# Division right behind the second products, GpSimd's subtractions in quarters, one-hot rows in one instruction, routing's rows of steps waiting by name

## The chip, the cores and the metric

The kernel runs on one core of one Trainium2 chip. Its time is the device time of one execution in microseconds (us). A core has engines that each run their own instructions in order and wait for one another through semaphores. TensorE (PE) does matrix products and transposes, VectorE (DVE) and ScalarE (ACT) work element by element, GpSimd (POOL) does the same and issues the gathers and scatters, and SyncE (SP) issues the other transfers (DMA). Loading of weights into TensorE is shown as PEld.

## The reference, cut to what matters

The first half is an attention in which each position sees its neighbours at a distance under 16 and one summary for each of 24 blocks of 32 positions. The second half sends each of the 3072 resulting rows through one of eight experts. Which expert that is depends on the rows before it.

```
# attention: B, H, S, D = 4, 8, 768, 64
k_sum = k.reshape(B, H, 24, 32, D).max(axis=3)
v_sum = v.reshape(B, H, 24, 32, D).mean(axis=3)
scores = scale * [q @ k.T where |i - j| < 16, q @ k_sum.T + log(32)]
a = exp(scores - max); a = a / (sum(a) + 1e-9)
x = (a @ [v, v_sum]) as B, S, 512
# routing and experts: E = 8, F = 1024
logits = x @ w_gate; local = sigmoid(x @ w_local)
e = argmax(logits) where s == 0 or local < 0.5, else the expert of the row before
out = softmax(logits)[e] * (relu(x @ w1[e]) @ w2[e])
```

## The kernel before, in words

**Attention.** The 4 blocks (one for each batch element) have 4 pairs of heads each. Such a pair is handled in two groups of 3 x 128 queries, so there are 32 groups, counted by `G`. The loop in `attention` is a pipeline by hand: in one turn `s_mm(G)` computes the scores (L251, L257), `t_stage(G - 2)` transposes the exponentials of two groups earlier (L278), `a_mm(G - 3)` multiplies with the values (L289), and `s_exp(G)` finds the row maximum on DVE (`nm`, L264) and exponentiates on ACT (L268). `a_norm` divides by the sum of the weights in three DVE instructions (L300, L302, L304). It takes group `G - 4` and stands ahead of `nm` of the same turn. The product's result has a single buffer in PSUM (bank "a"), so `a_mm` of one group waits until `a_norm` of the group before has read it. GpSimd prepares the scaled key windows (L216), folds the values (L209), writes the key summaries (L219) and spreads the value summaries (L228). `sum_v` (L223) turns value sums that DVE made (L204).

**Routing.** When the rows of a block are complete, they are transposed and multiplied with the gate's weights (L450, L468), and a row of small DVE steps with a few PE steps between them finds each row's expert and its place in that expert's list. These rows of steps are Python generators. `small(n)` issues up to n steps from the first two of them between two parts of the attention; `flow(dt)` does the same during the experts' products, by planned times (`C_DVE` for a step on DVE, `C_LAT` for its latency, `C_LONG` for a long one). At the end of a block's steps six instructions write one-hot rows `A` of 128 x 128 (L581). They are weights of later matrix products: `early(j)` (L700) finds which rows the slots 2j and 2j + 1 hold, `early_p(j)` (L727) their gate weights, and `finish` does so for the other slots, first with a product for four slots (L852 with 8 columns), then one that makes the words for the experts' numbers (L917), one for 32 slots (L852 with 64 columns), and the gate weights of 36 slots (L938). Block 3's routing and `finish` stand beside the experts' first three pairs.

**Experts.** A slot is 128 rows of one expert; slots are worked on in pairs (pairs 0 to 2 are the early ones). The rows are gathered by an indirect DMA (L960), transposed (L971), and multiplied by w1 (96 products of "first" kind, L1015 to L1017) and w2 (48 of "second" kind, L988 to L990). Every operand is a sum of a high and a low part, hence three products for each. ACT casts the high part of a weight (`h`, L951), and DVE or GpSimd subtracts it from the weight for the low part (`l`, L954, pieces of 128 x 1024). The slots of the next pair are gathered and transposed during the second products of a pair. The result is scaled by the gate weight (L997, L1000) and scattered (L1001). A store whose gate weight has not been planned yet issues routing's steps until it has, at that place (`while self.have_p <= i: self.small(1, True)`).

The engines' orders are fixed when the program is built. Only the loading and splitting of an expert's weights from pair 3 on depends on values read at run time.

Of the kernel before, what the change touches and what calls it, by code (L numbers as in the profile page):

```python
# [57 lines left out]
C_T, C_PE, C_WAIT, C_LONG, C_DVE, C_LAT, AHEAD = 0.65, 0.8, 0.3, 0.9, 0.17, 0.05, 1.5  # L58
# [4 lines left out]
class Kernel:  # L63
    def __init__(self, ctx, tc, qT, kT, vT, vW, maskc, identc, wgc, w1, w2, c32c, cb16c, out):
# [3 lines left out]
        self.t, self.q = 0.0, 0.0  # L68
        self.qT, self.kT, self.vT, self.vW = qT, kT, vT, vW
# [74 lines left out]
    def attention(self, tick, last):  # L144
        nc, tc, ident = self.nc, self.tc, self.ident
        with ExitStack() as ctx:
# [45 lines left out]
            for load, n in ((load_k, 1), (load_q, 1), (load_v, 0), (load_w, 0), (load_v, 1), (load_w, 1), (load_q, 2)):  # L192
                load(n)
# [18 lines left out]
            def windows(n, eng=nc.gpsimd, t0=0, t1=NW):  # L212

                src = kp[n % 2][:, 64 * t0:64 * t0 + 1]
                win = bass.AP(src.tensor, src.offset, [src.ap[0], (64, t1 - t0), (1, WL)])
                eng.tensor_scalar(out=kb[n % 2][:, t0:t1, 0:WL], in0=win, scalar1=0.125, scalar2=1.0, op0=ALU.mult, op1=ALU.mult)  # L216
# [75 lines left out]
            def a_norm(G):  # L292
# [8 lines left out]
                self.small(1)  # L301
                nc.vector.reciprocal(out=dn, in_=dn)  # L302
                self.small(1)
# [8 lines left out]
            windows(0, nc.vector, 0, NW // 2)  # L312
# [6 lines left out]
            for G in range(last_g + LA):  # L319
# [8 lines left out]
                if G < last_g and G % GP == 0 and G:  # L328
                    sum_v(G // GP, self.spare[:, 1, 0:P])
# [3 lines left out]
                if LA + 1 <= G <= last_g:  # L333
                    a_norm(G - LA - 1)
                tick(G, 3)
                if G < last_g:
                    s_exp(G)
                    self.small(3)
# [6 lines left out]
                if LA <= G:  # L345
                    a_mm(G - LA)
                if G < last_g:
# [15 lines left out]
                    else:  # L363
                        if n == 0:
                            sum_v(0, self.bank("t")[:, 0:P])
# [4 lines left out]
                        spread_v(n)  # L370
# [3 lines left out]
                else:  # L374
                    a_norm(G - LA)
                tick(G, 1)
                if G < last_g:
                    self.small(4, True)
                else:
                    self.flow(C_T)  # L380
# [8 lines left out]
    def wait(self):  # L389
        while len(self.steps) > 1:  # L390
            yield "WAIT"
# [92 lines left out]
    def route(self, b):  # L484
# [56 lines left out]
        v.tensor_tensor_scan(out=s2, data0=c["keep"], data1=o2, initial=0.0, op0=ALU.mult, op1=ALU.add)  # L541
        yield "PE"
# [35 lines left out]
        for u in range(NU):  # L578
            if u % 2 == 0:
                yield "DVE"  # L580
            v.tensor_scalar(out=self.A[:, b * NU + u, :], in0=c["iota128"], scalar1=lanf[:, u:u + 1],  # L581
                            scalar2=None, op0=ALU.is_equal)
# [21 lines left out]
    def second(self):  # L604
# [15 lines left out]
        v.scalar_tensor_tensor(out=cnt, in0=self.er, scalar=2.0 * P, in1=cnt, op0=ALU.mult, op1=ALU.max)  # L620
        yield "DVE"
# [16 lines left out]
        v.tensor_scalar(out=self.adj[:, 2], in0=self.is1, scalar1=-2.0, scalar2=7.0, op0=ALU.mult, op1=ALU.add)  # L638

    def gate_p(self, b0, b1):  # L640
# [30 lines left out]
        for i in range(3):  # L671
            yield "DVE"
            v.tensor_copy(out=p3[:, :, i, 0], in_=r)
            if i < 2:
                yield "DVE"
                v.tensor_tensor(out=r, in0=r, in1=p3[:, :, i, 0], op=ALU.subtract)

    def early(self, j, ef=None, places=None):
# [3 lines left out]
        n = self.early_b(j) * NU  # L682
        ef, places = ef or self.e0f, places or (2.0 * j, 2.0 * j + 1)
# [20 lines left out]
        for i in range(2):  # L704
            yield "DVE"
            v.scalar_tensor_tensor(out=self.lb[:, 0:n], in0=in0[:, :, i], scalar=64.0, in1=self.lb[:, 0:n], op0=ALU.mult, op1=ALU.add)

# [43 lines left out]
    def finish(self):  # L751
# [5 lines left out]
        nci = wk.tile([P, E], I32, name="nci")  # L757
        q = wk.tile([P, E], F32, name="q")
# [166 lines left out]
        yield from self.gate_p(B - 1, B)  # L925
        n = SLOTS - EARLY
# [22 lines left out]
    def split(self, which, c0, c1, src, eng):  # L949
        hi, lo = self.hi[which][:, c0:c1], self.lo[which][:, c0:c1]  # L950
        self.nc.scalar.copy(out=hi, in_=src)  # L951
        if eng is self.nc.vector:
            self.dve(1.1)
        eng.tensor_tensor(out=lo, in0=src, in1=hi.bitcast(F32), op=ALU.subtract)  # L954
# [389 lines left out]
```

## Time and profile before

| | |
|---|---|
| median of 3 runs | 497.64 us (493.22 to 499.40) |
| the profiled execution | 497.38 us, its span 495.6 us |
| mean granted TensorE clock | 0.957 |
| PE, PEld busy | 448.0 us (90%), 389.0 us (78%) |
| DVE, ACT, POOL busy | 285.2 us (58%), 216.4 us (44%), 190.1 us (38%) |
| moved by DMA | 92.04 MB, 186 GB/s in the mean |

Times in the profile count from the span's first instruction. Busy shares are of the span. The granted clock is what the throttle allowed TensorE in a stretch of time, 1.00 being full speed. In a row of the timeline the first number is the start, the second the duration, and a bracket at the end shows how long the engine had sat idle and what ended that. In a row of waits the numbers are the total, the number of waits and the longest.

### The profile page before, as it was taken

The page shows a single profiled execution, that of the slowest core. Times are in us where ns is not written, and L with a number is a line of the kernel's source. Part 1 is how long each engine was busy: PE and PEld are TensorE (multiplying, and loading weights), DVE is VectorE, ACT ScalarE, POOL GpSimd, SP SyncE. Part 2 cuts the span into 40 slices and gives each one's busy share as a digit, 9 for nine tenths or more (in the row PEclk, how much of TensorE's full clock was granted, in tenths as well). Part 3 has the DMA queues.
Part 4 walks back from the last instruction along what each step waited for, and adds up shares of the span by engine and source line. Part 5 has one row for each costly group of instructions (what it writes and reads, how often), then busy time and mean ns, then how long its engine had stood idle before and what let it go on. Part 6 is the DMA issues. An engine that isn't in the chain of part 4 may idle for free. (4 is left out here: it accounts for less than half of the span.)

```text
span 495.6 us, 11918 instructions
## 1 busy us (share of the span) xinstructions
PE 448.0 (90%) x4400; PEld 389.0 (78%) x4400; DVE 285.2 (58%) x623; ACT 216.4 (44%) x478; POOL 190.1 (38%) x152
## 2 busy tenths in 40 slices
PE   6899988878779999889899999999999999999990
PEld 5687776767567789688799998989879898977980
DVE  4686698777663756965522223158686226777610
ACT  3698876677535322702110201054556116274500
POOL 2685553373401230631102111146477204566720
PEclk9799999979879999979999999999999999999996
DMA  8999799678212084016402010119498503847840
GB/s 317 404 370 375 285 321 395 239 256 341 88 56 75 1 296 173 21 65 231 197 1 85 23 65 28 58 43 323 145 324 280 197 33 110 309 165 253 291 162 26
DMA packets 23622, 92.04 MB, mean 186 GB/s; under 512 B 2927, under 2 KB 3567, under 8 KB 19440
## 3 DMA queue, kind: packets, MB, share of 16 engines
q1 hardware_dynamic: 18752, 76.11, 42.2%
q0 software_dynamic: 4640, 14.68, 8.7%
q8 instruction: 41, 0.67, 0.5%
q14 instruction: 45, 0.37, 0.2%
q10 hardware_dynamic: 144, 0.20, 0.1%
HBM read 78.40 MB, written 13.11 MB: 185 GB/s over the span
## 5 line engine op out<-in xcount | busy, mean ns | idle before, releaser
L1015 PE MATMUL bs<-xT,h 128*128 128x256 f32 x384 | 110.6, 288 | 0.0
L1016 PE MATMUL bs<-xT,h 128*128 128x256 f32 x384 | 109.5, 285 | 0.5 <-DVE xT L966 0.5
L1017 PE MATMUL bs<-xT,l 128*128 128x256 f32 x384 | 109.6, 285 | 0.1
L1021 ACT ACTIVATE hT<-bs 128x512 fp32r<-128x512 f32 x48 | 28.7, 598 | 131.8 <-PE bs L1017 127.7
L960 POOL DMA_INDIRECT xg<-x_dram,gidx x32 | 34.8, 1089 | 127.5 <-POOLq L1191 57.7
L988 PE MATMUL ba<-h,hT 128*128 128x512 f32 x192 | 77.7, 405 | 0.4
L1023 DVE SCALAR_TENSOR_TENSOR hT<-bs,hT 128x512 fp32r<-128x512 f32 x48 | 33.0, 690 | 77.7 <-ACT hT L1021 66.8
L1016 PEld LDWEIGHTS bs<-xT,h 128*128 128x128 f32 x384 | 74.5, 194 | 1.1 <-DVE xT L966 0.7
L990 PE MATMUL ba<-h,hT 128*128 128x512 f32 x192 | 75.1, 391 | 0.0
L989 PE MATMUL ba<-l,hT 128*128 128x512 f32 x192 | 75.0, 391 | 0.0
L1015 PEld LDWEIGHTS bs<-xT,h 128*128 128x128 f32 x384 | 74.5, 194 | 0.7 <-issue 0.2
L1017 PEld LDWEIGHTS bs<-xT,l 128*128 128x128 f32 x384 | 74.4, 194 | 0.5 <-DVE l L954 0.5
L954 DVE TENSOR_TENSOR l<-stg,h 128x1024 fp32r<-128x1024 f32 x35 | 67.9, 1949 | 11.3 <-ACT h L951 8.1
L268 ACT ACTIVATE pr<-bs,nm 128x120 f32<-128x120 f32 x192 | 52.0, 372 | 25.2 <-DVE nm L264 24.8
L951 ACT CAST h<-stg 128x1024 fp32r<-128x1024 f32 x56 | 57.2, 1052 | 11.3 <-PE ba L990 8.2
L954 POOL TENSOR_TENSOR l<-stg,h 128x1024 fp32r<-128x1024 f32 x21 | 51.4, 2467 | 20.4 <-ACT h L951 20.4
L1001 POOL DMA_INDIRECT out_dram<-yo,sidx x26 | 31.1, 1197 | 59.1 <-DVE yo L1000 40.2
L988 PEld LDWEIGHTS ba<-h,hT 128*128 128x128 f32 x192 | 36.1, 188 | 8.0 <-ACTq L1191 0.6
L289 PE MATMUL ba<-vw,pt 120*64 120x65 f32 x768 | 33.0, 241 | 10.3 <-DVE xs L304 5.9
L990 PEld LDWEIGHTS ba<-h,hT 128*128 128x128 f32 x192 | 36.0, 188 | 7.8
L289 PEld LDWEIGHTS ba<-vw,pt 120*64 120x64 f32 x768 | 28.9, 153 | 15.7 <-issue 11.6
L989 PEld LDWEIGHTS ba<-l,hT 128*128 128x128 f32 x192 | 36.2, 189 | 6.2
(236 smaller groups left out, 672.3 us busy)
## 6 DMA issues: line engine op xcount, KB each, us to landing
stg<-in_w SPq DMA_DIRECT2D x32, 1024.0 KB, 5.7
vw<-in_vW SPq DMA_DIRECT2D x16, 780.0 KB, 4.5
kp<-in_kT SPq DMA_DIRECT2D x16, 384.0 KB, 6.3
q<-in_qT SPq DMA_DIRECT2D x16, 384.0 KB, 6.7
vt<-in_vT SPq DMA_DIRECT2D x16, 384.0 KB, 7.3
x_dram<-xs SPq DMA_DIRECT2D x8, 768.0 KB, 9.9
wst<-in_w SPq DMA_DIRECT2D x8, 512.0 KB, 8.4
xg<-x_dram,gidx POOLq DMA_INDIRECT x32, 8.4
```

What stands on the lines that cost most here:

```text
L268: nc.scalar.activation(out=pr[:, h, u, :], in_=sp[:, h, u, :], func=AF.Exp, bias=nm[:, h, u:u + 1], scale=1.0)
L289: nc.tensor.matmul(out=ap[64 * c:64 * c + 64, u, h, :], lhsT=pt[:, h, u, 64 * c:64 * c + 64], rhs=vw[n % 3][0:W, 2 * (NG * g + u) + c, h, ...
L951: self.nc.scalar.copy(out=hi, in_=src)
L954: eng.tensor_tensor(out=lo, in0=src, in1=hi.bitcast(F32), op=ALU.subtract)
L960: self.nc.gpsimd.indirect_dma_start(out=t, out_offset=None, in_=rows, in_offset=bass.IndirectOffsetOnAxis(ap=self.gidx[:, i:i + 1], axis=0))
L988: nc.tensor.matmul(out=ps, lhsT=ah, rhs=wh, start=first, stop=False)
L989: nc.tensor.matmul(out=ps, lhsT=ah, rhs=wl, start=False, stop=False)
L990: nc.tensor.matmul(out=ps, lhsT=al, rhs=wh, start=False, stop=last)
L1015: nc.tensor.matmul(out=ps[:, j], lhsT=wh, rhs=xh, start=(k == 0), stop=False)
L1016: nc.tensor.matmul(out=ps[:, j], lhsT=wh, rhs=xl, start=False, stop=False)
L1017: nc.tensor.matmul(out=ps[:, j], lhsT=wl, rhs=xh, start=False, stop=(k == KT - 1))
L1023: nc.vector.scalar_tensor_tensor(out=l, in0=ps, scalar=0.0, in1=h.bitcast(F32), op0=ALU.max, op1=ALU.subtract)
```

## The change

In the attention, `a_norm(G - 3)` now stands right behind `a_mm(G - 3)`, and no routing steps are slipped between its three instructions. `small` issues 3 + 2 + 3 steps in a turn, where it was 3 + 2 + 4 and the two of `a_norm`. The value sums of the first pair of heads are turned in the turns 2 and 3, and half of the first key windows is scaled by ACT. The one-hot rows of a block become one instruction of 128 x 768, which the planner counts as long. A GpSimd subtraction of 128 x 1024 becomes four of 128 x 256. Four planned costs are larger. Rows of steps wait by name (`until`) for what other rows of steps have done.

```
-C_T, C_PE, C_WAIT, C_LONG, C_DVE, C_LAT, AHEAD = 0.65, 0.8, 0.3, 0.9, 0.17, 0.05, 1.5
+C_T, C_PE, C_WAIT, C_LONG, C_DVE, C_LAT, AHEAD = 0.65, 0.8, 0.3, 1.1, 0.19, 0.1, 1.5
...
-            for load, n in ((load_k, 1), (load_q, 1), (load_v, 0), (load_w, 0), (load_v, 1), (load_w, 1), (load_q, 2)):
+            for load, n in ((load_k, 1), (load_v, 0), (load_q, 1), (load_w, 0), (load_v, 1), (load_w, 1), (load_q, 2)):
...
+                if eng is nc.scalar:
+                    eng.activation(out=kb[n % 2][:, t0:t1, 0:WL], in_=win, func=AF.Copy, scale=0.125)
...
                 nc.vector.tensor_scalar(out=dn, in0=ap[:, :, :, D:D + 1], scalar1=1e-9, scalar2=None, op0=ALU.add)
-                self.small(1)
                 nc.vector.reciprocal(out=dn, in_=dn)
-                self.small(1)
...
-                if LA + 1 <= G <= last_g:
-                    a_norm(G - LA - 1)
+                if G in (2, 3):
+                    sum_v(G - 2, self.bank("t")[:, 0:P])
+                    spread_v(G - 2)
...
-                    self.small(3)
+                    self.small(3, True)
...
                     a_mm(G - LA)
+                    a_norm(G - LA)
...
-                        spread_v(n)
+                        if n > 1:
+                            spread_v(n)
...
-                    self.small(4, True)
+                    self.small(3, True)
...
+    def until(self, *names):
+        while not self.done.issuperset(names):
+            yield "WAIT"
...
+        yield from self.until(("counts", b))
...
-        for u in range(NU):
-            if u % 2 == 0:
-                yield "DVE"
-            v.tensor_scalar(out=self.A[:, b * NU + u, :], in0=c["iota128"], scalar1=lanf[:, u:u + 1],
-                            scalar2=None, op0=ALU.is_equal)
+        if b < B - 2:
+            self.done.add(("counts", b + 1))
+        yield "LONG"
+        v.tensor_tensor(out=self.A[:, ts, :], in0=c["iota128"].unsqueeze(1).to_broadcast([P, NU, P]),
+                        in1=lanf.unsqueeze(2).to_broadcast([P, NU, P]), op=ALU.is_equal)
...
+        yield from self.until(("early", j - 1))
...
+            yield from self.until(("weights", 0))
...
+        yield from self.until("second", ("early", EARLY // 2 - 1))
...
+        yield from self.until(("weights", 0), ("weights", 2))
...
         if eng is self.nc.vector:
-            self.dve(1.1)
-        eng.tensor_tensor(out=lo, in0=src, in1=hi.bitcast(F32), op=ALU.subtract)
+            self.dve(1.4)
+            eng.tensor_tensor(out=lo, in0=src, in1=hi.bitcast(F32), op=ALU.subtract)
+            return
+        for o in range(0, c1 - c0, 256):
+            p = slice(o, o + 256)
+            eng.tensor_tensor(out=lo[:, p], in0=src[:, p], in1=hi[:, p].bitcast(F32), op=ALU.subtract)
```

The orders of the engines show where routing's steps have gone. The line numbers of the changed kernel are its own: L700 has become L712, L727 L741, L852 L867, L917 L932, L938 L954, L960 L981, L971 L992, L954 L970 on DVE and L975 on POOL, and the second products are L1009 to L1011.

PE before, in the second products of pair 0 (L988 to L990, the result in `ba`): the product for the slots 2 and 3 (L700, 18 pieces) and the transposes of slot 2's gathered rows (L971), with 27 second products between them, of which four are shown.

```order
L700 MATMUL bt<-ebt_2965,A 128x4
L988 MATMUL ba<-h_115,hT 128x512
...
L512 MATMUL bt<-ident,val 6x128
...
L518 MATMUL bt<-ident,pm 128x6
L988 MATMUL ba_3106<-h_115,hT 128x512
L989 MATMUL ba_3106<-l_117,hT 128x512
L990 MATMUL ba_3106<-h_115,hT 128x512
...
L971 MATMUL bt<-ident,xg_118 128x128 x4
```

The same place of the changed kernel.

```order
L519 MATMUL bt<-ident,val 6x128
...
L712 MATMUL bt<-ebt_3014,A 128x4
L1009 MATMUL ba_3039<-h_115,hT 128x512
L1010 MATMUL ba_3039<-l_117,hT 128x512
L1011 MATMUL ba_3039<-h_115,hT 128x512
L525 MATMUL bt<-ident,pm 128x6
L992 MATMUL bt<-ident,xg_118 128x128 x4
```

The product has moved 24 second products back, behind `val` of the next block's routing (L512, now L519), and 3 second products are left between it and the transposes of the rows whose numbers it finds.

DVE before, at the end of the first products of pair 1: the operands of the gate weights' product for the slots 2 and 3 (`ebp_3340`), its result (L730), and the first subtraction of the next weights (`l_116`, L954).

```order
L723 TENSOR_TENSOR ebp_3340<-p_85,ein_2962 128x18x3
L791 TENSOR_SCALAR bi<-bi 128x8
L723 TENSOR_TENSOR ebp_3340<-p_85,ein_2962 128x18x3
L1023 SCALAR_TENSOR_TENSOR hT<-bs,hT 128x2x256
...
L730 TENSOR_REDUCE psort<-bt 128x2
...
L954 TENSOR_TENSOR l_116<-stg_3002,h_114 128x1024
```

DVE of the changed kernel, at the second products of pair 1. Between the third subtraction (L970) and the second `ebp_3420` stand 27 rows of gate weights (`ex`, `sm`, `gr`, `p`) and of `finish` (`nbi`, `q`, `cum`), nearly all of 8 to 48 elements.

```order
L970 TENSOR_TENSOR l_116<-stg_2990,h_114 128x1024
L987 TENSOR_TENSOR xT<-bt,xT 128x4x128
L970 TENSOR_TENSOR l_116<-stg_2990,h_114 128x1024
L662 TENSOR_TENSOR ex_3365<-l_all,gmx_3100 128x48
...
L737 TENSOR_TENSOR ebp_3420<-p_85,ein_3003 128x18x3
L813 TENSOR_SCALAR s_3422<-pc 128x8
L737 TENSOR_TENSOR ebp_3420<-p_85,ein_3003 128x18x3
...
L744 TENSOR_REDUCE psort<-bt 128x2
L970 TENSOR_TENSOR l_117<-stg_2991,h_115 128x1024 x2
```

The operands have moved from ahead of the subtractions to behind three of them and behind the second transposed slot (`xT`). PE's product that reads them (L741) now stands behind the first 24 second products of pair 1; before it stood behind 90 of the 96 first products.

PE before, from the middle of pair 2's second products to its end: the product for 32 slots (L852), slot 7's transposes, and the gate weights (L938).

```order
L852 MATMUL bt<-bt_3719,A 128x64
L988 MATMUL ba<-h_115,hT 128x512
...
L971 MATMUL bt<-ident,xg_119 128x128 x4
...
L1191 UNCONDITIONAL_BRANCH x8
L938 LDWEIGHTS A
L938 MATMUL bt<-bp,A 128x108
```

PE of the changed kernel at the end of pair 2.

```order
L1011 MATMUL ba_3826<-h_115,hT 128x512
L1212 UNCONDITIONAL_BRANCH x8
L867 LDWEIGHTS A
L867 MATMUL bt<-bt_3877,A 128x64
...
L954 LDWEIGHTS A
L954 MATMUL bt<-bp,A 128x108
L1036 MATMUL bs<-xT,h_114 128x256
```

The product for 32 slots has moved behind the last second product of pair 2, so that only its own 24 pieces stand between that and the gate weights' product, and the first products of pair 3 (L1036) follow. DVE's part between the two has kept its 22 instructions: five for the numbers, thirteen for the gate weights, one `eqp` and three `bp`. The product for four slots (L867 with 8 columns) and the words' product (L932) now stand next to one another behind the first 3 second products of pair 2; between those two DVE has 25 instructions.

More of the change, by code (lines that the diff above doesn't have):

```diff
@@ L68, in __init__ @@
         self.t, self.q = 0.0, 0.0
+        self.done = {("counts", 0), ("early", -1)}
         self.qT, self.kT, self.vT, self.vW = qT, kT, vT, vW
@@ L215, in windows @@
                 win = bass.AP(src.tensor, src.offset, [src.ap[0], (64, t1 - t0), (1, WL)])
-                eng.tensor_scalar(out=kb[n % 2][:, t0:t1, 0:WL], in0=win, scalar1=0.125, scalar2=1.0, op0=ALU.mult, op1=ALU.mult)
+                if eng is nc.scalar:
+                    eng.activation(out=kb[n % 2][:, t0:t1, 0:WL], in_=win, func=AF.Copy, scale=0.125)
+                else:
+                    eng.tensor_scalar(out=kb[n % 2][:, t0:t1, 0:WL], in0=win, scalar1=0.125, scalar2=1.0, op0=ALU.mult, op1=ALU.mult)
             def summaries(n, eng=nc.gpsimd):
@@ L311, in attention @@
             reduce_k(0)
-            windows(0, nc.vector, 0, NW // 2)
+            windows(0, nc.scalar, 0, NW // 2)
             windows(0, nc.gpsimd, NW // 2, NW)
@@ L327, in attention @@
                 tick(G, 2)
-                if G < last_g and G % GP == 0 and G:
+                if GP < G < last_g and G % GP == 0:
                     sum_v(G // GP, self.spare[:, 1, 0:P])
@@ L364, in attention @@
                         if n == 0:
-                            sum_v(0, self.bank("t")[:, 0:P])
                             reduce_v(1)
@@ L373, in attention @@
                             load_q(n + 3)
-                else:
-                    a_norm(G - LA)
                 tick(G, 1)
                 if G < last_g:
-                    self.small(4, True)
+                    self.small(3, True)
                 else:
@@ L620, in second @@
         v.scalar_tensor_tensor(out=cnt, in0=self.er, scalar=2.0 * P, in1=cnt, op0=ALU.mult, op1=ALU.max)
+        self.done.add(("counts", B - 1))
         yield "DVE"
@@ L638, in second @@
         v.tensor_scalar(out=self.adj[:, 2], in0=self.is1, scalar1=-2.0, scalar2=7.0, op0=ALU.mult, op1=ALU.add)
+        self.done.add("second")
     def gate_p(self, b0, b1):
@@ L676, in gate_p @@
                 v.tensor_tensor(out=r, in0=r, in1=p3[:, :, i, 0], op=ALU.subtract)
+        self.done.add(("weights", b0))
     def early(self, j, ef=None, places=None):
@@ L706, in early @@
             v.scalar_tensor_tensor(out=self.lb[:, 0:n], in0=in0[:, :, i], scalar=64.0, in1=self.lb[:, 0:n], op0=ALU.mult, op1=ALU.add)
+        self.done.add(("early", j))
     def early_b(self, j):
```

## The prediction

> **What bounds the kernel now.** I read the page first: shares of busy time, then the granted clock by slices.
>
> ```profile
> PE 448.0 (90%) x4400; PEld 389.0 (78%) x4400; DVE 285.2 (58%) x623; ACT 216.4 (44%) x478; POOL 190.1 (38%) x152
> PEclk9799999979879999979999999999999999999996
> ```
>
> TensorE is the bound, so a term counts only as it makes PE idle or slower. The stretches say where that is. After start and end come PE's busy time, the other engines', the granted clock, DMA share and GB/s.
>
> ```profile
> 80.00:150.00 70.00, 55.28 (x897) 45.19 (x887) 51.30 (x152) 41.38 (x124) 27.32 (x23) 0.85 0.59 213
> 250.00:480.00 230.00, 226.69 (x1420) 202.59 (x1420) 113.75 (x107) 84.14 (x110) 91.50 (x59) 1.00 0.45 155
> ```
>
> From 250 to 480 us PE is busy for 226.7 of 230 us at full clock: little can be won there, and what DVE and GpSimd do is hidden. From 80 to 150 us, the attention with routing beside it, PE is idle for 14.7 us, and a clock of 0.85 costs up to 55.28 x 0.15 = 8.3 us more. The list of PE's waits names the causes.
>
> ```profile
> PE ba L289 <- DVE xs L304: 5.9, 5, 2.5
> PE bt L852 <- DVE bt L848: 4.8, 1, 4.8
> PE ba L289 <- issue: 2.7, 2, 2.3
> PE bt L938 <- DVE bp L934: 2.5, 1, 2.5
> PE bs L257 <- POOL kb L219: 2.0, 1, 2.0
> PE bt L512 <- DVE dn L302: 2.0, 2, 1.0
> PE bt L700 <- DVE ebt L696: 1.9, 1, 1.9
> ```
>
> **What the attention gets back.** L289 waits for xs (5.9 us) because the division of a group runs one turn later, with routing's steps ahead of it and inside it, and the products have one buffer. With the division right behind the product, its three instructions have a whole turn. L512 is a routing step on PE whose operand stood among them; it is now behind the product: 2.0 us go. The "issue" wait of 2.3 us comes where the division stands behind six one-hot instructions.
>
> ```profile
> L581 DVE TENSOR_SCALAR A<-c,lanf 128x128 bf16<-128x128 f32 x24 | 11.7, 543 | 0.0
> 225.95 0.93 DVE L843 TENSOR_TENSOR eq<-c,blk 128x768 f32<-128x768 f32 x1
> L954 POOL TENSOR_TENSOR l<-wst,h 128x1024 fp32r<-128x1024 f32 x4 | 9.5, 2370 | 40.4 <-issue 28.5 <-ACT h L951 11.9
> L209 POOL TENSOR_TENSOR vf<-vt 128x384 f32<-128x384 f32 x14 | 14.2, 1011 | 8.1 <-DMA vt<-in_vT 4.5 <-DVE va L204 2.4 <-DVE cnt L553 1.2
> ```
>
> Six of these are 6 x 0.54 = 3.3 us; the nearest row with two operands and 128 x 768 elements takes 0.93, so one instruction is some 0.9 to 1.2 us, and the 2.3 us go too. L700's 1.9 us may go, since it is a turn later, or move; I take 1.0. Together 5.9 + 2.0 + 2.3 + 1.0 = 11.2 us back.
>
> Against it, GpSimd's quarters. No row shows 128 x 256. Four cannot be under the 2.37 us of the whole, nor, by the row of 128 x 384, much over 4 x 1.01 = 4.0. Between these two rows an element costs (2.37 - 1.01) / 640 = 2.1 ns, which leaves 0.2 us for each instruction; so I take 4 x (0.54 + 0.2) = 3.0. One such subtraction stands ahead of the key summaries for which L257 waits 2.0 us, and it grows by 0.6. Net **-10.6 us**. The ends: -14 if small waits that I don't count go as well, and -5 if the routing products that may now stand behind the exponentials (`small(3, True)`) make PE wait instead.
>
> Clock next.
>
> ```profile
> 85.00:90.00 5.00, 5.00 (x73) 4.10 (x74) 2.03 (x5) 2.32 (x8) 1.01 (x1) 0.69 0.63 249
> 105.00:110.00 5.00, 3.67 (x37) 3.48 (x36) 4.83 (x11) 2.83 (x9) 4.12 (x5) 0.52 0.40 136
> ```
>
> The low stretches follow the waits: 0.69 behind the 2.3 us wait that ends at 84.9, 0.52 behind the two of 2.0 and 1.3 at 102 to 107, of which the first stays. I take some half of the 8.3 us, **-4.2**, between 0 and -8.
>
> By the Trainium skill's "TensorE: Matmul & The Clock Gate", Part 1 (what's actually happening), the clock halves after an idle window of about 3.4 us, and as much busy time restores it. The row at 85 does not agree: the clock was 0.69 behind a shorter idle time. By the rule alone nothing would come back here (a rival below).
>
> **The start.** GpSimd's order changes where the loads still rule.
>
> ```profile
> 19.06 1.02 POOL L209 TENSOR_TENSOR vf<-vt 128x384 f32<-128x384 f32 x1 [0.72 <-DMA vt<-in_vT]
> 20.04 0.44 POOL L219 TENSOR_SCALAR kb<-ks 128x288 f32<-128x288 f32 x1
> 20.54 1.46 POOL L228 COPY vw<-vs 24x1536 f32<-24x1536 f32 x1
> 20.53 0.85 PE L257 MATMUL bs<-kb,q 64*64 64x120 f32 x24
> ```
>
> The summaries of pair 2 end at 20.48, and L257 starts at 20.53. The changed order puts the spread of 1.46 us ahead of them: **+1.5**. PE waits there for the summaries in both orders, so nothing hides it. The ends are 0, if the folding comes earlier, and +3.
>
> **The experts' first pairs.** Here routing's products have moved back. Pair 0: L700 now has 3 second products behind it before L971 reads what the gather brings.
>
> ```profile
> 170.97 0.39 PE L990 MATMUL ba<-h,hT 128*128 128x512 f32 x1
> 171.20 0.61 PE L700 MATMUL bt<-ebt,A 128*128 128x4 bf16 x18
> 173.17 0.98 POOL L960 DMA_INDIRECT xg<-x_dram,gidx  x1 [3.51 <-DVE lb L706]
> 178.44 0.60 PE L971 MATMUL bt<-ident,xg 128*128 128x128 f32 x4
> ```
>
> A second product takes 0.23 us (170.97 to 171.20), so 27 of them hid 6.2 us, and 3 hide 0.7. From L700's end at 171.81 to the gather's start were 1.4 us, and at 178.44, 6.6 us after L700, the rows were there. PE loses at most 6.6 - 0.7 = 5.9 us; the gather's own 0.98 us and the 1.4 ahead of it give at least 1.7. I take **+4.0**, nearer the upper end, since the landing comes on top of the second figure.
>
> Pair 1: L727 for the slots 2 and 3 is forced behind 24 second products by the store that needs its result, with 28 small DVE steps ahead of its operands, and these behind the third subtraction.
>
> ```profile
> 195.45 0.28 PE L1015 MATMUL bs<-xT,h 128*128 128x256 f32 x1
> 195.68 0.28 PE L1017 MATMUL bs<-xT,l 128*128 128x256 f32 x1
> 204.83 1.21 DVE L954 TENSOR_TENSOR l<-stg,h 128x1024 fp32r<-128x1024 f32 x1
> 201.13 2.04 DVE L823 TENSOR_SCALAR o<-pt 128x24 int32<-128x24 int32 x1
> 207.83 2.34 DVE L835 CAST_PREDICATED blk<-e,pt 128x24 f32<-128x24 int32 x1
> 206.77 3.35 POOL L954 TENSOR_TENSOR l<-stg,h 128x1024 fp32r<-128x1024 f32 x1 [1.56 <-ACT h L951]
> 238.00 0.17 DVE L676 TENSOR_TENSOR gr<-gr,p 128x6 f32<-128x6 f32 x1
> 238.61 0.17 DVE L673 CAST p<-gr 128x6 bf16<-128x6 f32 x1
> ```
>
> First products end at 195.8. 24 second products (5.5 us) and two of L971 (1.2) later PE is at L727, 6.7 us on. The third subtraction ended at 206.0, 10.2 us on, but behind an instruction held for 2.04 us; without that, and without the steps that the change puts behind it, it is some 7 us on. Dependent small steps follow one another every 0.2 us (three from 238.00 to 238.61): 28 are 5.6 us. So 12.6 - 6.7 = 5.9; I take **+5.8**, between 3 (if the casts come early) and 8.
>
> The held steps bear on pair 2. Beside GpSimd's subtraction, 24 elements took 2.34 us, where 0.2 is usual. With quarters such a step should wait for some 0.75 us at most.
>
> The Trainium skill's "SBUF — State Buffer", Who interferes with whom, says that DVE and GpSimd share a port pair as an exclusive lock for a whole instruction. The rows agree. By the rule, the shorter lock would spare pair 2's chain two waits of some 1.6 us each, which the sum below has already left out with L852's old wait.
>
> Pair 2: L852 with 8 columns and L917 now stand side by side behind 3 second products. L852 misses its operands by some 1.8 us (the last hT, two small steps, then 0.9 for `eq` and `bt`, less 0.7), and L917 then waits for 25 steps, 5.2 us. That is 7.0 instead of the 4.8 of L852: **+2.2**, between -2 and +4.
>
> End of pair 2: L852 with 32 slots, and L938 behind it with no product between.
>
> ```profile
> 230.75 0.87 PE L852 MATMUL bt<-bt,A 128*128 128x64 bf16 x24
> 231.96 0.19 DVE L740 COPY tl<-bt 128x32 f32<-128x32 f32 x1 [0.40 <-PE bt L852]
> 238.69 1.05 DVE L929 TENSOR_TENSOR eqp<-c,blk 128x864 f32<-128x864 f32 x1
> 239.77 3.00 DVE L934 TENSOR_TENSOR bp<-eqp,p 128x864 bf16<-128x864 f32 x3
> 242.83 1.34 PE L938 MATMUL bt<-bp,A 128*128 128x108 bf16 x24 [2.47 <-DVE bp L934]
> ```
>
> Behind L852's end come 0.4 us, 18 small steps (3.8), `eqp` (1.05) and three `bp` (3.0): 8.3 to 8.5 us in which PE has nothing, instead of 2.47. **+6.0**, between +4 (a few steps overlapped) and +9.
>
> And the clock behind each of the three new long waits. Before, behind L852's 4.8 us:
>
> ```profile
> 215.18 0.41 PE L1015 MATMUL bs<-xT,h 128*128 128x256 f32 x1
> 215.39 0.41 PE L1016 MATMUL bs<-xT,h 128*128 128x256 f32 x1
> ```
>
> A first product every 0.21 us, where 0.12 is usual (195.45 to 195.68 is two), for about 3.8 us: 1.6 us lost. Three times that is **+4.8**, between 2 and 6.
>
> From pair 3 on I cost the quarters at nothing: PE's 226.7 of 230 us hide them. Without the cover it is 0.6 us for a subtraction.
>
> **Sum.** +1.5 - 10.6 - 4.2 + 4.0 + 5.8 + 2.2 + 6.0 + 4.8 = +9.5 against the profiled run's 497.38 us; the small pieces of the attention that I left out of -10.6 (waits under 1 us) I put at -0.7. That gives **506.2 us**. The profiled run is 0.26 us under the median shown, so no correction is made.
>
> **Rivals.** *The attention wins* (faster): its waits and clock come back whole, -14 and -8, and the experts' chains take their lower ends, since DVE is no longer held beside GpSimd: 1.5 - 22 + 1.7 + 3 - 2 + 4 + 2 = -12, 485.6 us. It decides if the new PE waits in pairs 0 to 2 stay under about 12 us together. For it speaks that all its gaps are seen, while mine are worked out from an order; against it, that L938 has nothing to stand beside. *The waits move inside the attention* (slower): routing products ahead of L289 now wait for DVE's longer rows, the gain halves to -7, and the rest stands: +24.3 - 7 = +17.3, about 515 us. *The clock stays low*: the low stretches have a cause other than waits of 1 to 2 us; then the -4.2 is missing and the time is some 510 us. The row at 85 speaks against it, that at 105, with a wait that stays, does not. *The change does not do it*: DVE's steps reach PE no later than before, because DVE is idle while PE is busy, and the gains of the attention are used up by one new wait: 497 us.
>
> **How the numbers follow.** The sum has 0.44, the attention's win 0.16, the waits inside it 0.18, the low clock 0.08, and no effect 0.14. Its own range is 500 to 512; with the ends of the rivals I say 491 to 517. 2% (10 us) is about what a measurement of this kernel can tell from no change. The forecast lies at +1.7%, so its share falls on both sides of 507.6: 0.26 within, 0.18 over. Faster by over 2% is most of the first rival, 0.15; within 0.26 + 0.14 + 0.01 = 0.41; slower 0.18 + 0.18 + 0.08 = 0.44.
>
> **What would show it.** Right: no waits of L289 for xs over 1 us; a wait of L971 for the gather in pair 0, of L727 in pair 1, of L917 in pair 2, and 8 us at L938; first products at 0.21 us behind each. Wrong: a PE without idle time at these four places, or waits of L289 as before. GpSimd's quarters would be wrong at a mean far from 0.75 us.

## The result, and the profile after

The changed kernel takes **518.07 us** (median of 4, 517.32 to 518.29), the kernel before beside it 497.81: a ratio of 1.042, 95% interval 1.035 to 1.049. It is slower by 20.3 us, where 8.8 was forecast; the time lies 1 us above the range. The profiled execution took 517.97 us, its span is 516.2.

The first rows of the page, as before: busy shares, then the granted clock.

```profile
PE 450.6 (87%) x4400; PEld 391.5 (76%) x4400; DVE 252.9 (49%) x602; ACT 217.1 (42%) x479; POOL 213.0 (41%) x227
PEclk9799999989998899697969999999999999999996
```

PE does the same work (450.6 us, 448.0 before) in a longer span. DVE is busy 32 us less and GpSimd 23 us more. The low clock has moved from the attention to the stretch from about 155 to 270 us.

Where the first product of a pair of slots starts parts the span into stages. These rows of PE's timeline are of before, then of after: pairs 0, 1, 2 and 3.

```profile
147.46 0.39 PE L1015 MATMUL bs<-xT,h 128*128 128x256 f32 x1
183.67 0.36 PE L1015 MATMUL bs<-xT,h 128*128 128x256 f32 x1
213.75 0.56 PE L1015 MATMUL bs<-xT,h 128*128 128x256 f32 x1
243.98 0.36 PE L1015 MATMUL bs<-xT,h 128*128 128x256 f32 x1
```

```profile
139.54 0.38 PE L1036 MATMUL bs<-xT,h 128*128 128x256 f32 x1
184.56 0.28 PE L1036 MATMUL bs<-xT,h 128*128 128x256 f32 x1
219.61 0.28 PE L1036 MATMUL bs<-xT,h 128*128 128x256 f32 x1
264.40 0.56 PE L1036 MATMUL bs<-xT,h 128*128 128x256 f32 x1
```

The attention (up to pair 0) is 7.9 us shorter. Pair 0 is 8.8 us longer (45.0 instead of 36.2), pair 1 5.0 us, pair 2 14.6 us. From pair 3 on both take 251.6 to 251.8 us. So 28.4 us were lost in three pairs and 7.9 gained ahead of them. What the 7.9 us are, PE's busy time up to pair 0 shows, before and then after (the columns are those of the prediction's stretches):

```profile
0.00:147.46 147.46, 124.70 (x2216) 101.69 (x2216) 106.11 (x283) 100.48 (x317) 70.10 (x73) 0.91 0.78 286
0.00:139.54 139.54, 116.67 (x2203) 95.03 (x2203) 99.95 (x263) 100.96 (x318) 71.56 (x79) 0.96 0.83 301
```

PE is idle there for 22.8 us before and for 22.9 after. So in sum no waiting was won in the attention: the 7.9 us are busy time, at a granted clock of 0.96 instead of 0.91. In the three pairs PE is idle for 9.8 us before and 28.8 after, and busy 9.4 us longer. The list of PE's waits after the change:

```profile
PE bt L954 <- DVE bp L950: 8.0, 1, 8.0
PE bs L227 <- DVE va L205: 7.5, 8, 1.7
PE bs L261 <- POOL kb L223: 7.4, 2, 5.2
PE bt L741 <- DVE ebp L737: 5.8, 1, 5.8
PE bt L992 <- DMA xg<-x_dram,gidx: 5.1, 2, 3.9
PE bt L932 <- DVE tot L926: 4.7, 1, 4.7
PE bs L255 <- ACT pr L272: 3.7, 3, 1.9
PE bt L867 <- DVE bt L863: 1.8, 1, 1.8
```

All the waits for the divided rows (xs) are gone, and so is the one of the old L700. In the three pairs stand the four waits that were forecast, of almost the sizes that were forecast. Three were not: eight of L227 for the value sums, one of 5.2 us of L261 at the start, and three of L255 for the exponentials (pr), also at the start, where before L223 waited 4.9 us for the value sums. The stretches behind the four long waits have these clocks (the third figure from the end; the first after the bounds is the length, the second PE's busy time):

```profile
175.00:180.00 5.00, 2.66 (x9) 2.27 (x10) 0.86 (x3) 0.59 (x1) 0.94 (x1) 0.62 0.38 105
180.00:185.00 5.00, 5.00 (x21) 4.09 (x20) 1.58 (x11) 0.82 (x2) 0.00 (x0) 0.69 0.00 0
210.00:215.00 5.00, 4.22 (x27) 3.45 (x28) 1.03 (x10) 1.46 (x2) 1.01 (x1) 0.50 0.14 52
215.00:220.00 5.00, 5.00 (x21) 4.06 (x20) 1.69 (x2) 2.56 (x4) 2.08 (x3) 0.78 0.01 2
240.00:245.00 5.00, 5.00 (x18) 3.95 (x16) 0.72 (x3) 0.59 (x1) 0.78 (x1) 0.55 0.55 175
260.00:265.00 5.00, 2.71 (x27) 2.72 (x28) 2.50 (x4) 0.00 (x0) 0.00 (x0) 0.50 0.00 0
265.00:270.00 5.00, 5.00 (x31) 5.00 (x31) 0.00 (x0) 0.60 (x1) 0.00 (x0) 0.66 0.00 0
```

Busy time times what the clock lacks is 1.0 + 1.6 behind the gather's wait, 2.1 + 1.1 behind L741's, 2.3 behind L932's and 1.4 + 1.7 behind L954's: 11.1 us in all.

### The profile page after: what moved, and what is told of

The parts are those of the page before. It is cut to its first block, busy times and chain, and to the rows that moved or that the text cites. A ratio compares the mean times of both kernels' runs of the same rounds, so it can differ in the third digit from the quotient of the medians.

```text
span 516.2 us, 11970 instructions
## 1 busy us (share of the span) xinstructions
PE 450.6 (87%) x4400; PEld 391.5 (76%) x4400; DVE 252.9 (49%) x602; ACT 217.1 (42%) x479; POOL 213.0 (41%) x227
## 5 line engine op out<-in xcount | busy, mean ns | idle before, releaser
L1036 PE MATMUL bs<-xT,h 128*128 128x256 f32 x384 | 111.2, 290 | 0.0
L981 POOL DMA_INDIRECT xg<-x_dram,gidx x32 | 37.7, 1177 | 132.3 <-POOLq L1212 54.7
L1009 PE MATMUL ba<-h,hT 128*128 128x512 f32 x192 | 80.3, 418 | 0.4
L975 POOL TENSOR_TENSOR l<-stg,h 128x256 fp32r<-128x256 f32 x84 | 73.4, 909 | 12.3 <-issue 6.3
L1010 PE MATMUL ba<-l,hT 128*128 128x512 f32 x192 | 77.4, 403 | 0.0
L1011 PE MATMUL ba<-h,hT 128*128 128x512 f32 x192 | 77.2, 402 | 0.0
L1036 PEld LDWEIGHTS bs<-xT,h 128*128 128x128 f32 x384 | 75.0, 195 | 0.7 <-issue 0.2
L967 ACT CAST h<-stg 128x1024 fp32r<-128x1024 f32 x56 | 57.1, 1051 | 14.1 <-PE ba L1011 13.2
L970 DVE TENSOR_TENSOR l<-stg,h 128x1024 fp32r<-128x1024 f32 x35 | 46.1, 1327 | 23.8 <-ACT h L967 20.8
L1022 POOL DMA_INDIRECT out_dram<-yo,sidx x26 | 26.8, 1032 | 65.7 <-DVE yo L1021 21.3
L1009 PEld LDWEIGHTS ba<-h,hT 128*128 128x128 f32 x192 | 37.7, 196 | 8.6 <-ACTq L1212 0.6
L1011 PEld LDWEIGHTS ba<-h,hT 128*128 128x128 f32 x192 | 37.6, 196 | 8.4
L1010 PEld LDWEIGHTS ba<-l,hT 128*128 128x128 f32 x192 | 37.8, 197 | 6.6
L985 ACT CAST xT<-bt 128x512 fp32r<-128x512 f32 x27 | 15.6, 587 | 50.7 <-PE bt L992 49.4
L987 DVE TENSOR_TENSOR xT<-bt,xT 128x512 fp32r<-128x512 f32 x27 | 18.5, 689 | 33.3 <-ACTq L1212 22.6
## 6 DMA issues: line engine op xcount, KB each, us to landing
wst<-in_w SPq DMA_DIRECT2D x8, 512.0 KB, 6.2
```

The lines of the kernel that those rows point to most:

```text
L975: eng.tensor_tensor(out=lo[:, p], in0=src[:, p], in1=hi[:, p].bitcast(F32), op=ALU.subtract)
L981: self.nc.gpsimd.indirect_dma_start(out=t, out_offset=None, in_=rows, in_offset=bass.IndirectOffsetOnAxis(ap=self.gidx[:, i:i + 1], axis=0))
L1009: nc.tensor.matmul(out=ps, lhsT=ah, rhs=wh, start=first, stop=False)
L1010: nc.tensor.matmul(out=ps, lhsT=ah, rhs=wl, start=False, stop=False)
L1011: nc.tensor.matmul(out=ps, lhsT=al, rhs=wh, start=False, stop=last)
L1036: nc.tensor.matmul(out=ps[:, j], lhsT=wh, rhs=xh, start=(k == 0), stop=False)
```

## The experiments

Every run was compared with runs of the kernel before on the same chip. "First products" is where pair 0's start in the profiled execution, "three pairs" the time from there to the start of pair 3's; both are read from PE's timeline as above. The changed kernel and e4 have the same attention, and their first products start 3.0 us apart; a difference of that size in this column, from one profile each, says little.

| run | time us | ratio to before (95%) | first products | three pairs |
|---|---|---|---|---|
| before (profile) | 497.4 | | 147.5 | 96.5 |
| changed | 518.1 | 1.042 (1.035 to 1.049) | 139.5 | 124.9 |
| e1 old places | 497.0 | 1.002 (0.999 to 1.005) | 153.7 | 92.9 |
| e2 old costs | 500.9 | 1.010 (1.007 to 1.013) | 141.2 | 106.1 |
| e3 old steps | 518.6 | 1.044 (1.040 to 1.049) | 153.6 | 111.3 |
| e4 warm | 512.0 | 1.030 (1.024 to 1.035) | 142.6 | 118.7 |
| e5 division at its old place | 514.8 | 1.037 (1.034 to 1.041) | 139.1 | 121.0 |
| e6 division behind the sums | 513.9 | 1.036 (1.032 to 1.040) | 139.2 | 123.2 |
| e7 quarters alone | 490.0 | 0.988 (0.984 to 0.992) | 144.3 | 94.7 |
| e8 old start | 514.6 | 1.038 (1.032 to 1.044) | 138.3 | 124.8 |
| e9 new costs alone | 509.8 | 1.028 (1.023 to 1.032) | 145.2 | 109.3 |
| e10 lower costs | 476.3 | 0.961 (0.957 to 0.965) | 132.0 | 91.8 |
| e11 lower costs, six one-hot | 479.3 | 0.967 (0.962 to 0.973) | 136.1 | 91.7 |
| e12 lowest costs | 476.6 | 0.960 (0.955 to 0.965) | 131.4 | 94.1 |

The theory to be tried first was that of the prediction: routing's products stand too late on TensorE, and PE waits for chains that have nothing beside them. Its rival: the operations themselves (quarters, the longer one-hot instruction) slow DVE's chains down.

**e1, e2, e3: what moved the places.**

```
# e2: the changed kernel with
-C_LONG, C_DVE, C_LAT = 1.1, 0.19, 0.1     self.dve(1.4)
+C_LONG, C_DVE, C_LAT = 0.9, 0.17, 0.05    self.dve(1.1)
# e3: the changed kernel with
                 nc.vector.tensor_scalar(out=dn, ...)
+                self.small(1)
                 nc.vector.reciprocal(out=dn, in_=dn)
+                self.small(1)
...
-                    self.small(3, True)    # behind s_exp
+                    self.small(3)
...
-                    self.small(3, True)    # end of the turn
+                    self.small(4, True)
# e1: both, and the six one-hot instructions instead of one
```

Expected of e1: 

> The changed kernel with the planner's old costs, the old number of steps in a turn and the six one-hot instructions again; routing's products then stand on TensorE at the places of the kernel before, while the division behind the products, GpSimd's quarters, the start and the waits by name stay. If the 28 us lost between pair 0's and pair 3's start come from the places of the products: about 490 us (497.8 less the 8 us that the attention gained), with L954 (the gate weights) waiting some 2.5 us again. If they come from the quarters or from the longer chains themselves: over 505 us.

Expected of e2: 

> The changed kernel with the planner's four old costs alone. The product for slots 2 and 3 then has 12 second products behind it instead of 3, the product for four slots moves into pair 2's first products, and the words' product, L741 in pair 1 and the end of pair 2 keep their places. If the places decide: the gather's wait falls from 3.9 to about 2, L867's 1.8 goes, L932's 4.7 falls below 2, the 5.8 and 8.0 stay; about 508 us. If the costs of the plan do not matter: 518 us.

Expected of e3: 

> The changed kernel with the old number of steps in a turn of the attention alone (two inside the division, four at the end, none of the first three on TensorE). The product for slots 2 and 3 has 15 second products behind it instead of 3, the rest of the experts' places hardly move. If the places decide: the gather's wait falls from 3.9 to about 1, L741's 5.8, L932's 4.7 and L954's 8.0 stay; about 513 us, less if the attention's waits for the divided rows come back. If the steps in a turn are what matters most: below 505 us.

The four costs alone take 17 of the 20 us away, more than expected. PE's waits of e2, for the four late products and the gathered rows:

```profile
PE bt L954 <- DVE bp L950: 7.9, 1, 7.9
PE bt L741 <- DVE ebp L737: 3.2, 1, 3.2
PE bt L992 <- DMA xg<-x_dram,gidx: 1.7, 1, 1.7
PE bt L867 <- DVE bt L863: 1.4, 1, 1.4
PE bt L932 <- DVE tot L926: 1.1, 1, 1.1
```

From 25.4 us these waits have come down to 15.3; only the one at the end of pair 2 is left whole, as its place did not move. The clock comes back with them: the three pairs are 18.7 us shorter, 10 of it waits.

e3 shows a trade: with the old number of steps the attention is 14.1 us longer and the three pairs 13.6 us shorter, and the sum is the same (518.6 us, where 513 was expected). So the 7.9 us that the changed attention is shorter than the old one hang on the steps, and they are paid back behind it. Whether it is their number or their places in the turn, two of them inside the division, e3 does not tell.

e1 has the old places, and its three pairs are even 3.6 us shorter than before, but its attention is 6.2 us longer. So half of the expectation failed: the loss is that of the places, but the gain of the attention did not stay, because it had been the steps'. PE's longest wait of e1 in the attention, for the value sums:

```profile
PE bs L227 <- DVE va L205: 10.9, 9, 2.8
```

**e9: the new costs alone**, on the kernel before, with the waits by name: 

> The kernel before with the planner's four new costs and the waits by name (which keep routing's rows of steps in a legal order under them), nothing else of the change. If the costs make the loss: the first products start near 147 as before, L741, the words and the gate weights wait some 6, 5 and 8 us, the three pairs take 115 to 125 us instead of 96.5, and the time is 513 to 520 us. If the loss needs the fewer steps, the quarters or the one-hot instruction too: below 506 us.

```
# the kernel before with `until` and
-C_LONG, C_DVE, C_LAT = 0.9, 0.17, 0.05    self.dve(1.1)
+C_LONG, C_DVE, C_LAT = 1.1, 0.19, 0.1     self.dve(1.4)
```

It is 13.3 us slower, in the three pairs alone (109.3 instead of 96.5 us). That lies between the two values expected: below the 513 us from which the theory counted, and above its rival's 506. Three of the four waits are there:

```profile
PE bt L958 <- DVE bp L954: 7.9, 1, 7.9
PE bt L936 <- DVE tot L930: 4.7, 1, 4.7
PE bt L745 <- DVE ebp L741: 4.5, 1, 4.5
```

The fourth, for the gathered rows, is missing: 18 second products stand between the product for the slots 2 and 3 and the transposes. So the costs alone, without the quarters and the one-hot instruction, make 12.8 of the 28.4 us that were lost in the pairs; for the rest the fewer steps are needed too (e3 takes 13.6 us back). The rival falls: these waits come without the two operations, and e7 and e11 will show that each of the two wins time.

**e4: what the clock costs.** The waits are filled with products of zeros.

```
+    def warm(self, m, n):
+        for _ in range(n):
+            self.nc.tensor.matmul(out=m[:, 0:P], lhsT=self.wz, rhs=self.wz, start=True, stop=True)
...
             m = self.bank("t")
+            self.warm(m, 90 if j == 1 else 0)     # early_p; 60, 24, 72 and 128 at the four others
```

Expected: 

> The changed kernel with idle products of zeros on TensorE ahead of the five late products (60 before the gathered rows of slot 2, 90 before L741, 24 before the product for four slots, 72 before the words, 128 before the gate weights), which fill most of each wait; their result is overwritten. If the low clock behind these waits costs some 11 us, as the granted clock after them suggests: about 508 us. If the clock has another cause, or its loss is the 1.6 us a wait that the prediction took: 513 to 518 us.

PE is kept busy, and behind three of the waits the clock stays up. Behind the fourth, the gathered rows of slot 2, 2.12 us of idle time were left, and it fell to 0.66 (the first row):

```profile
180.00:185.00 5.00, 4.86 (x20) 4.13 (x21) 1.43 (x7) 0.58 (x1) 0.00 (x0) 0.66 0.00 1
205.00:220.00 15.00, 14.19 (x150) 12.43 (x150) 9.53 (x40) 7.19 (x10) 7.63 (x8) 1.00 0.05 19
240.00:245.00 5.00, 5.00 (x29) 4.16 (x27) 1.05 (x3) 0.86 (x2) 1.04 (x2) 1.00 0.53 174
260.00:270.00 10.00, 9.90 (x97) 9.90 (x97) 1.70 (x4) 1.19 (x2) 0.00 (x0) 1.00 0.00 0
```

The time falls by 6.1 us (to 512.0), the three pairs by 6.2. In PE's timeline, the first of the 60 idle products ahead of slot 2 and the transposes of the slots 2 and 4:
```profile
174.50 1.68 PE L132 MATMUL bt<-wz 128*128 128x128 bf16 x27
180.14 0.66 PE L1001 MATMUL bt<-ident,xg 128*128 128x128 f32 x4 [2.12 <-DMA xg<-x_dram,gidx]
203.17 0.66 PE L1001 MATMUL bt<-ident,xg 128*128 128x128 f32 x4 [2.29 <-DMA xg<-x_dram,gidx]
```

6.1 us is more than 1.6 for each of three waits (4.8) and less than 11.1. A part of the rest shows in the waits for the gathered rows, which grew: in slot 4 from 1.20 to 2.29 us, and in slot 2 from 3.9 to 5.6 us, from the first idle product at 174.50 to 180.14. In slot 2 the rows themselves came later, 6.5 us behind the product of their numbers (L712 in the changed kernel) instead of 4.9; why was not tried and stays open.

**e5, e6: the division's place.**

```
# e5: the changed kernel with a_norm(G - LA - 1) ahead of s_exp again, no steps inside
# e6: the changed kernel with
                     a_mm(G - LA)
-                    a_norm(G - LA)
...                                       # folds, summaries, reduce_v of the turn
+                if LA <= G:
+                    a_norm(G - LA)
                 tick(G, 1)
```

Expected of e5: 

> The changed kernel with the division at its old place (a turn later, ahead of the row maximum), still without steps inside it. If the new place is what gave the attention back its waits, as the prediction has it: the first products start later than the 139.5 us of the changed kernel, near 147, and the time is about 525 us. If fewer steps in a turn gave it, and the new place itself costs (TensorE waits 0.67 us a pair for the value sums, whose reduction now stands on DVE behind the division): the waits of L227 for va go, the first products start near 134, and the time is about 512 us.

Expected of e6: 

> The changed kernel with the division in the same turn, but behind the reduction of the value sums in DVE's order. If the division ahead of the reduction makes TensorE wait for va: these waits (7.5 us in 8) go, and the time is about 511 us. If the reduction waits for GpSimd's folding: the waits stay, 518 us.

With the division at its old place the first products start at 139.1 us, as with the new one (139.5); neither 147 nor 134 came. So the new place gained nothing; what the attention gained hangs on the steps (e3). The waits for xs that come back with the old place are 4.9 us in four, and the 7.5 us for va go:

```profile
PE ba L293 <- DVE xs L306: 4.9, 4, 1.5
```

In the changed kernel, in the clean stretch at 30 us, DVE and PE do this:

```profile
29.67 0.56 DVE L306 TENSOR_TENSOR xs<-ba,dn 128x384 f32<-128x384 f32 x1
30.15 0.54 DVE L205 TENSOR_REDUCE va<-vf 128x24 f32<-128x384 f32 x1
30.75 0.28 PE L227 MATMUL bs<-ident,va 128*24 128x128 f32 x1 [0.67 <-DVE va L205]
```

DVE waits for PE's product of this turn, divides, and only then reduces the value sums, which PE wants right behind the next scores. In e6 the reduction stands ahead of the division (which starts at 35.62), and L227 does not wait:

```profile
35.14 0.54 DVE L205 TENSOR_REDUCE va<-vf 128x24 f32<-128x384 f32 x1
36.41 0.28 PE L227 MATMUL bs<-ident,va 128*24 128x128 f32 x1
```

From the scores of group 5 to those of group 12 PE takes 21.07 us before, 22.80 changed, 21.13 in e5 and 20.92 in e6: the new place cost 0.25 us a turn there. Of the whole time e6 returns 4.1 us, less than the 7 expected: other waits take their place (L520 for val 2.4 us, L553 for sc 1.6). The row maximum of group 25 still starts 3.2 us earlier than in the changed kernel (100.97 and 104.19 us), that of group 30 only 0.5 (129.44 and 129.90). By the ratios to before, e5 and e6 are 0.5 and 0.6% below the changed kernel, and the intervals overlap, so neither gain is clear of the noise.

**e7: the quarters alone.**

```
# the kernel before with, for GpSimd,
+        for o in range(0, c1 - c0, 256):
+            eng.tensor_tensor(out=lo[:, o:o+256], in0=src[:, o:o+256], in1=hi[:, o:o+256].bitcast(F32), op=ALU.subtract)
```

Expected: 

> The kernel before with GpSimd's subtractions in quarters, nothing else; all orders stay but for the quarters. If the small steps that DVE held for 2.0 to 2.3 us beside GpSimd made L852 wait 4.8 us: that wait falls below 1, no such step takes over 1 us, and the time is about 493 us. If the quarters' own cost shows (L257 waiting 2.6 instead of 2.0, later gathers): 497 us or more.

Of the two parts that were tried alone (e7, e9), this one pays: 490.0 us, 1.2% faster (interval 0.8 to 1.6). This row of DVE's timeline is the counterpart of the one that took 2.34 us before:

```profile
205.69 0.73 DVE L835 CAST_PREDICATED blk<-e,pt 128x24 f32<-128x24 int32 x1
```

And these are the groups of both engines' subtractions (busy time, mean ns of one, idle time ahead), two rows of before and two of e7:

```profile
L954 POOL TENSOR_TENSOR l<-stg,h 128x1024 fp32r<-128x1024 f32 x21 | 51.4, 2467 | 20.4 <-ACT h L951 20.4
L954 DVE TENSOR_TENSOR l<-stg,h 128x1024 fp32r<-128x1024 f32 x35 | 67.9, 1949 | 11.3 <-ACT h L951 8.1 <-ACTq L1201 2.4 <-DVEq L1201 0.6
L957 POOL TENSOR_TENSOR l<-stg,h 128x256 fp32r<-128x256 f32 x84 | 73.5, 910 | 15.4 <-ACT h L951 15.3
L957 DVE TENSOR_TENSOR l<-stg,h 128x1024 fp32r<-128x1024 f32 x35 | 46.7, 1344 | 16.2 <-ACT h L951 12.9 <-ACTq L1204 2.4 <-DVEq L1204 0.6
```

PE's wait of L852 in the list of waits:

```profile
PE bt L852 <- DVE bt L848: 1.9, 1, 1.9
```

In the three pairs no small step of DVE (up to 108 elements) takes over 0.8 us, its own subtractions fall from 1949 to 1344 ns in the mean, and L852's wait from 4.8 to 1.9 us, though not below 1. 0.91 us for a quarter beside the experts is more than the 0.75 estimated (beside the attention 0.73), and PE's list of waits has none for it.

**e8: the start.**

```
# the changed kernel with the first loads as before, windows(0) on DVE,
# sum_v and spread_v of the first pair of heads in the turns 0 and 1
```

Expected: 

> The changed kernel with the old start (order of the first loads, first windows on DVE, first value sums in the turns 0 and 1). If the spread ahead of the summaries costs the 3.6 us by which the sixth group's scores start later: these start near 23, L261 loses its wait of 5.2 us, and the time is about 515 us. If the loads rule the start in any order: 518 us.

```profile
20.41 1.46 POOL L232 COPY vw<-vs 24x1536 f32<-24x1536 f32 x1
22.44 1.48 PE L261 MATMUL bs<-kb,q 64*64 64x120 f32 x24 [5.21 <-POOL kb L223]
```

These rows are the changed kernel's. With the old start the wait of 5.2 us goes, the scores of group 5 start at 24.8 us instead of 26.6 (23 was expected), and the first products 1.2 us earlier. The run changes the loads and the first windows back too, so the spread is not parted from them. The time is 3.4 us less, but its runs spread over 511.7 to 517.4, so its size stays unclear.

**e10, e11, e12: the parts that pay, with places that fit.** Two costs below the old ones (the latency and DVE's subtraction), two as they were; the division behind the sums; the old start.

```
# e10: e6 with the old start (e8) and
-C_LONG, C_DVE, C_LAT = 1.1, 0.19, 0.1     self.dve(1.4)
+C_LONG, C_DVE, C_LAT = 0.9, 0.17, 0.0     self.dve(1.0)
# e11: e10 with the six one-hot instructions
# e12: e10 with 0.8, 0.16, 0.0 and self.dve(0.9)
```

Expected of e10: 

> The changed kernel with planned costs lower than the old ones (a small step 0.17, latency 0, a long one 0.9, DVE's subtraction 1.0), the old start, and the division behind the value sums in the same turn. The product for slots 2 and 3 then has 24 second products behind it, the words' product stands in pair 2's first products, the product for 32 slots six first products before their end. If the places made the loss: first products near 138 us, three pairs in about 95 us, the gate weights waiting under 2 us; about 486 us. If DVE's chain is the limit and the earlier places only turn into waits for DVE: about 500 us.

Expected of e11: 

> As the run with lower costs, with the six one-hot instructions again (the places on TensorE are within 12 products of that run's). If the single instruction is worth what DVE's time says, 2 us for each of four blocks where something waits for it: 2 to 4 us slower than that run. If the fewer steps in a turn hide it: the same time within 1 us.

Expected of e12: 

> As the run with lower costs, with a small step at 0.16, a long one at 0.8 and DVE's subtraction at 0.9: the product for 32 slots 30 first products earlier, the gate weights 6 second products before the end of pair 2. If places are what is left to win: L954's wait goes and the time is 1 to 2 us below that run. If DVE's small steps take 0.2 us in truth, TensorE waits at the earlier places instead: 1 to 5 us above it.

e10 takes 476.3 us, 3.9% less than before, 10 us under what was expected. PE's longest waits of it:

```profile
PE bt L227 <- DVE va L205: 3.2, 1, 3.2
PE bt L930 <- DVE w L921: 2.5, 1, 2.5
```

And its product for the gate weights in the timeline:

```profile
222.59 1.34 PE L952 MATMUL bt<-bp,A 128*128 128x108 bf16 x24 [0.30 <-DVE bp L948]
```

The gate weights wait 0.3 instead of 8.0 us, and the three pairs take 91.8 us, 33.1 less than in the changed kernel. The first products start at 132.0 us; that is 7.6 us earlier than with all of the change, while the division's place (e6) and the start (e8) brought 0.3 and 1.2 each. Here waiting did go: PE is idle for 14.5 us up to the first products (busy 117.44 of 131.95), where it was 22.9. Why the two bring more together was not tried and stays open.

The six one-hot instructions cost 3.0 us (479.3), within what the single instruction was said to be worth; every run of e11 is longer than every run of e10. e12 is like e10 (the intervals cover one another), so neither value expected came: earlier places than e10's win nothing, and L930, the words' product, waits 2.9 us instead of 2.5.

## Why the prediction was right or wrong, point by point

- **The waits in the three pairs: right, one by one.** Gather: 3.9 us for slot 2 against 4.0; L741 5.85 against 5.8; L867 and L932 together 6.5 against 7.0; L954 7.98 against 8.3 to 8.5. Together they grew by 17.0 us, where 18.0 was forecast; a gather's wait of 1.2 us in pair 1, which was not forecast, makes it 18.2. Rows of order, laid against durations of before, gave this; no row of the changed kernel was needed.
- **The clock behind them: mis-sized.** The term was 4.8 us, 1.6 for each of three waits. The granted clock says 11.1 behind four, and 2.2 behind the old L852 (1.91 x 0.40 + 5.00 x 0.28, from 210 to 220 us of before): 8.9 more. I had counted L932's wait as the old L852's, and I had taken the loss from the 3.8 us in which first products came every 0.21 us, where one or two whole stretches of 5 us stayed at 0.50 to 0.78. Keeping PE busy (e4) gave 6.1 us back net of gathers that then were waited for longer.
- **The attention's waits: the step that failed.** I put -10.6 for waits, -0.7 for small ones and +1.5 for the start, together -9.8, and -4.2 for the clock: -14.0. It was -7.9, and none of it was waiting: PE was idle for 22.8 us before and 22.9 after. The waits for xs did go, but others took their place: 7.5 us of L227, and 5.2 of L261 and 3.7 of L255 at the start. The step "its three instructions have a whole turn" looked at who waits for the division and not at what stands behind it on DVE: the value sums, for which L227 waited. They are not the whole of it, since e6 took these waits away and the first products came only 0.3 us earlier; what else holds the attention stays open. e5 shows that the new place gained nothing in sum, and e3 that the gain hangs on the steps in a turn, which the prediction priced at nothing, except as places behind.
- **The attention's clock: right in direction, too small.** PE's busy time fell by 8.0 us, where -4.2 was forecast (by stretches of 5 us, the loss to the clock from 20 us to the first products fell from 8.5 to 3.1 us). Part of this was luck: the term counted on waits that go, and the idle time stayed as long. It lies at other places now; whether the clock rose for that is not shown. The same attention in e4 was busy 2.8 us longer.
- **What the miss is made of.** The profiled time moved by 20.6 us instead of 8.8. Of the 11.8 us between, 9.9 are the attention's waits, 4.6 the clock in the three pairs and 0.9 the waits there; the attention's clock gave 3.8 more than forecast, and 0.2 lie behind the pairs.
- **The start: 1.5 was the spread itself.** GpSimd's rows agree (1.46 us ahead of the summaries, L261 at 22.44 us against 20.53). But PE then came out of 5.2 us of waiting with a low clock (0.90 from 20 to 50 us), and group 5's scores started 3.5 us later.
- **The quarters: the sign was wrong.** I priced them at +0.6 in the attention and nothing from pair 3 on, and left their gain for DVE in L852's term alone. By themselves they make the kernel 1.2% faster (e7): 3.2 us of it in the attention and 1.8 in the three pairs by the profiled executions, of which the first is about what two profiles of one attention differ by. A quarter took 0.73 us beside the attention and 0.91 beside the experts, where 0.75 was the estimate.
- **The rivals.** "The waits move inside the attention" came nearest (515 us), but by another mechanism: the reduction behind the division and the start, not routing's products ahead of L289. "The clock stays low" was wrong: in the attention the clock did come back.
- **The clock's rule and the port's.** The 0.50 to 0.78 in the stretches of the four long waits show a low clock behind idle time, and e4, which kept PE busy, shows that the idle time is its cause. The Trainium skill's "TensorE: Matmul & The Clock Gate", Part 1 (what's actually happening), names an idle window of about 3.4 us ahead of the half clock and as much busy time to undo it. The four long waits agree with the first. The second is short here: behind L954 the first products still came every 0.21 us at 268.0 us, 5.7 us after PE had started again (262.29). The 0.69 behind a wait of 2.3 us before does not fit a bare threshold, nor does the 0.66 from 155 to 160 us of the changed kernel, where no wait of the 14 us ahead is over 0.73 us. For the port, the step that took 2.34 us before takes 0.73 with the same work in quarters. The Trainium skill's "SBUF — State Buffer", Who interferes with whom, describes the lock held for a whole instruction, and this agrees. For this change it was worth more than the sum gave it.

## What to carry to other kernels

When an instruction is moved to shorten one wait, list what is queued behind it on its engine and who waits for that: here the division, moved ahead of the value sums, put a wait for these in place of the waits it removed. PE's idle time, added up over the stage before and after, shows whether waits went or only moved. Planned costs that are too high are not a safe side: they put products late, where nothing stands beside the chain they wait for, and each long wait is paid again by the clock behind it. And when a change has many parts, the order that comes out of the plan tells more of its time than the cost of any operation; much the same operations took 518 us with one table of costs and, with two places mended, 476 with another.

## What the runs showed of the hardware that was not expected

- A wait of 4 to 8 us cost TensorE 2.3 to 3.2 us more behind it by the granted clock, against 1.6 estimated from the spacing of products.
- The granted clock can fall without a long wait: it was 0.66 from 155 to 160 us of the changed kernel, and no wait of PE in the 14 us ahead was over 0.73 us.
- A GpSimd subtraction of 128 x 256 took 0.73 us beside the attention and 0.91 beside the experts, so four are 2.9 to 3.6 us, where one of 128 x 1024 took 2.37 to 2.47. DVE gained about as much as GpSimd lost: 67.9 - 46.7 = 21.2 us on its own subtractions (e7), while GpSimd's rose from 51.4 to 73.5, by 22.1 us, for which PE did not wait; over the whole run DVE was busy 23.4 us less and GpSimd 22.5 more.
